# Text queries and keys by column groups, and one double-width load, in a joint image and text attention block

## The chip, the cores and the metric

The kernel runs on one core of a Trainium2 chip. The metric is device time in microseconds (us) of one execution, taken as the median of several. A core has a matrix engine (TensorE, in the profile PE, with its weight loads as PEld), VectorE (DVE), ScalarE (ACT), GpSimd (POOL) and SyncE (SP), which here only issues transfers. Work that goes on together on several engines is ordered by semaphores. TensorE reads from the on-chip memory SBUF (128 partitions) and adds up in eight PSUM banks; VectorE and ScalarE move the sums back to SBUF. Sixteen DMA engines carry data from and to the device memory.

## The reference

Two batches of 256 image tokens and 32 text tokens, width D = 1152, all in bfloat16. Image and text have weights of their own, and meet in one softmax:

```python
mod_i = (_silu(c) @ wmod_img).reshape(B, 6, 1, D)      # shift, scale, gate are the first three
hi = _layernorm(x_img) * (1 + sci) + shi               # ht likewise from x_txt, wmod_txt
qi, ki, vi = split(hi @ wqkv_img)                      # qt, kt, vt likewise from ht, wqkv_txt
q = concat([qt, qi], axis=1)                           # k, v likewise
p = softmax(q @ k.T * D ** -0.5)
at, ai = split(p @ v)
out_i = x_img + gai * (ai @ wo_img)
out_t = x_txt + gat * (at @ wo_txt)
```

## The kernel before

Contractions run over D in KT = 9 blocks of 128 rows. Every weight matrix of 1152 by 1152 lies in SBUF as a tile of 128 partitions by 9 by 1152 (2.65 MB), loaded by SP in one to three pieces (`load_w`, line 73). The tiles share a pool of five slots (line 54); a new matrix takes the slot whose earlier readers are done first. The order of all instructions is written out by hand, each engine and each transfer queue runs its own list in that order, and the loads are issued long ahead: from line 433 on they stand as image keys, text shift, text scale, text tokens, text queries, text keys, image gate (in the place of the image values' weights), text values, image output, text gate, text output.

The stages on TensorE, in order: the image values (`va`), the image shift, the image queries (`qk_img` with `w_q_i`), the image keys (`qk_img` with `w_k_i`), the scores, the text values and gates, the transposed probabilities, the attention's output (`aps`), and the output products (L826 for the image, L799 and L844 for the text).

`qk_img` makes one column block of 128 at a time: nine matmuls over kt, 128 weight columns against 512 image tokens, into one PSUM bank, whose result is cast into `qkTs[blk]`, features on the partitions and tokens along the row. The text work is woven into the image keys by hooks, run ahead of a column block: at 3 the text layer norm, at 6 the strips of text shift and scale (`row_strips`), at 7 the transposes of the text tokens, at 8 the text queries. The text keys follow behind block 8, and then the scores begin (`scores_img`, line 590, one tile for each batch and half of the image queries, over nine feature blocks of image and text keys together; then the text queries' own scores in `scores_txt_and_gate`).

`qk_txt` (line 559) holds 128 columns of the weights still and streams the 64 text tokens past, 81 matmuls for each of queries and keys; two PSUM tiles, one of six and one of three column blocks, are copied out each time.

`mod_strip` (line 399) is the other form that the kernel has for such small products: here the few rows (32) are held still, and the weights stream past. Four matmuls go to four column groups of the array at once, group g with 288 of the 1152 weight columns, and write 32 PSUM partitions each. `strip_cols` then transposes the 128 by 288 result in blocks of 32 by 32 on VectorE, after which partition 32g+j of block m holds feature 128m+32g+j.

PSUM's eight banks are a pool of seven that all matmul results take in turn, and one for small results.

## Time and profile before

| | us |
|---|---|
| median of 3 runs | 114.88 |
| lowest to highest | 114.66 to 114.92 |
| the profiled execution | 114.55 |
| its span, first to last instruction | 112.7 |

The profile is of one execution. Its page gives each engine's busy time and number of instructions, the span cut into 40 slices of 2.8 us (each digit the busy share in tenths), the chain of work that ended last, followed back from the last instruction, and the costliest groups of instructions. A group's row reads: line, engine, operation, output and inputs, shape, count, then busy time, mean duration of one in ns, and the idle time ahead of it. The timeline lists start, length and count of like instructions in a row. Matmuls overlap: one lasts longer than the step to the next, so a row's length contains the last one's tail, and steps are worked out from starts. A few matmul records can be missing.

### The profile page before, as it was taken

The page shows a single profiled execution, that of the slowest core. Times are in us where ns is not written, and L with a number is a line of the kernel's source. Part 1 is how long each engine was busy: PE and PEld are TensorE (multiplying, and loading weights), DVE is VectorE, ACT ScalarE, POOL GpSimd, SP SyncE. Part 2 cuts the span into 40 slices and gives each one's busy share as a digit, 9 for nine tenths or more (in the row PEclk, how much of TensorE's full clock was granted, in tenths as well). Part 3 has the DMA queues.
Part 4 walks back from the last instruction along what each step waited for, and adds up shares of the span by engine and source line. Part 5 has one row for each costly group of instructions (what it writes and reads, how often), then busy time and mean ns, then how long its engine had stood idle before and what let it go on. Part 6 is the DMA issues. An engine that isn't in the chain of part 4 may idle for free.

```text
span 112.7 us, 2837 instructions
## 1 busy us (share of the span) xinstructions
PE 107.6 (95%) x1182; PEld 64.1 (57%) x1191; DVE 76.2 (68%) x151; ACT 36.5 (32%) x83; POOL 28.1 (25%) x62
## 2 busy tenths in 40 slices
PE   5989999999999999999999999999999999999990
PEld 1356665565544444444446558787687565667670
DVE  1699330865499999999999950238657700899971
ACT  4527500471280080730009933024647700001000
POOL 7000120830230000000000161601540460499600
PEclk9999999999999999999999999999999999999999
DMA  3999999999999999999999999999999999994052
GB/s 90 321 376 347 373 373 407 409 413 411 405 410 408 411 410 413 404 412 410 413 410 414 413 403 408 404 398 404 410 407 401 411 422 394 383 371 168 7 192 70
DMA packets 22839, 40.87 MB, mean 363 GB/s; under 512 B 1375, under 2 KB 6635, under 8 KB 22827
## 3 DMA queue, kind: packets, MB, share of 16 engines
q1 hardware_dynamic: 21547, 39.05, 90.4%
q10 hardware_dynamic: 672, 0.77, 2.2%
q0 software_dynamic: 608, 0.88, 2.2%
q8 instruction: 9, 0.15, 0.5%
q14 instruction: 3, 0.02, 0.1%
HBM read 39.36 MB, written 1.34 MB: 361 GB/s over the span
## 4 chain that ended last, share of the span: by engine, by line
PE 89%; DVE 4%; DMA 3%; ACT 1%; issue 1%; ACTq 0%
PE qkps L504 31%; PE ps L826 16%; PE va L256 14%; PE aps L734 5%; PE ps L565 4%; PE sps L594 4%; PE gps L404 3%; DMA x_i<-in_x_img_dram 3%; DVE stats L166 3%; PE ops L844 2%; PE van L268 2%; PE ps L669 2%; PE mps L218 1%; ACT hT_i L202 1%; PE gps L799 1%; PE sps L607 1%
## 5 line engine op out<-in xcount | busy, mean ns | idle before, releaser
L504 PE MATMUL qkps<-hT_i,t 128*128 128x512 bf16 x158 | 35.4, 379 | 0.2
L504 PEld LDWEIGHTS <-t 128*128 128x128 bf16 x162 | 15.6, 98 | 18.7 <-DMA t<-in_wqkv_img_dram 0.3
L466 DVE SCALAR_TENSOR_TENSOR sacc<-w_v_i,mcols,sacc 128x1152 f32<-128x1152 bf16 x16 | 22.7, 1418 | 0.5
L256 PE MATMUL va<-w_v_i,hT_i 128*128 128x512 bf16 x67 | 17.0, 379 | 0.4 <-issue 0.2
L826 PE MATMUL ps<-t,aT 128*128 128x384 bf16 x99 | 16.4, 326 | 0.0
L826 PEld LDWEIGHTS <-aT 128*128 128x128 bf16 x117 | 11.0, 98 | 6.9 <-issue 0.5
L832 DVE TENSOR_TENSOR tmp<-ps,gb 128x384 bf16<-128x384 f32 x11 | 6.0, 548 | 6.5 <-DMA gb<-mod_scratch 6.0
L810 POOL TENSOR_TENSOR w_og<-t,gb 128x384 bf16<-128x384 bf16 x9 | 8.7, 1007 | 5.2 <-DMA gb<-mod_scratch 5.2
L256 PEld LDWEIGHTS <-hT_i 128*128 128x128 bf16 x72 | 6.4, 97 | 5.8 <-issue 0.2
L523 POOL TENSOR_SCALAR mod_txt<-mcols 128x18 f32<-128x18 f32 x2 | 0.6, 275 | 32.4 <-DVE mcols L410 32.4
L166 DVE BATCH_NORM_STATS2 stats<-x_i 128x6 f32<-128x384 bf16 x12 | 5.8, 541 | 2.6 <-DMA x_i<-in_x_img_dram 2.6
L454 ACT ACTIVATE qT<-qkps 128x512 bf16<-128x512 f32 x9 | 4.7, 601 | 6.9 <-PE qkps L504 6.9
L140 PE MATMUL wps<-wz 128*128 128x512 bf16 x15 | 5.6, 536 | 1.2 <-DVE wz L125 1.2
L470 ACT CAST shi<-sacc 128x1152 bf16<-128x1152 f32 x2 | 2.3, 1152 | 13.2 <-DVE sacc L466 13.2
L241 POOL TENSOR_SCALAR hT_i<-hT_i,mod_img 128x128 bf16<-128x128 bf16 (+1 forms) x5 | 2.1, 437 | 14.9 <-ACT hT_i L202 8.5
L747 DVE TENSOR_SCALAR aT<-aps,sv 128x288 bf16<-128x288 f32 (+2 forms) x11 | 4.3, 455 | 2.0 <-PE aps L734 2.0
L833 DVE TENSOR_TENSOR o<-tmp,x_i 128x384 bf16<-128x384 bf16 x11 | 5.3, 479 | 0.4
L565 PEld LDWEIGHTS <-t 128*128 128x128 bf16 x162 | 5.0, 98 | 0.5
L154 DVE CAST kT<-qkps 128x512 bf16<-128x512 f32 x3 | 2.1, 686 | 4.7 <-PE qkps L504 4.7
L565 PE MATMUL ps<-hT_t,t 128*128 128x64 bf16 x162 | 5.0, 193 | 0.0
L734 PE MATMUL aps<-pT,v_i 128*128 128x288 bf16 (+2 forms) x44 | 4.8, 264 | 0.0
L749 ACT ACTIVATE aT<-aps,sv 128x288 bf16<-128x288 f32 (+2 forms) x11 | 4.0, 468 | 2.1 <-PE aps L734 2.1
(150 smaller groups left out, 141.6 us busy)
## 6 DMA issues: line engine op xcount, KB each, us to landing
t<-in_wqkv_img_dram SPq DMA_DIRECT2D x6, 864.0 KB, 13.7
t<-in_wmod_txt_dram SPq DMA_DIRECT2D x2, 2592.0 KB, 18.2
t<-in_wqkv_txt_dram SPq DMA_DIRECT2D x2, 1440.0 KB, 14.3
t<-in_wmod_img_dram SPq DMA_DIRECT2D x3, 864.0 KB, 11.7
t<-in_wqkv_txt_dram SPq DMA_DIRECT2D x3, 864.0 KB, 14.0
t<-in_wo_txt_dram SPq DMA_DIRECT2D x3, 864.0 KB, 15.3
t<-in_wqkv_txt_dram SPq DMA_DIRECT2D x2, 1152.0 KB, 15.0
w_v_i<-in_wqkv_img_dram SPq DMA_DIRECT2D x7, 288.0 KB, 6.7
```

Source lines behind the costliest of these rows:

```text
L140: nc.tensor.matmul(ps[:], lhsT=wz[:, 0:P], rhs=wz[:], start=True, stop=True)
L166: nc.vector.bn_stats(stats[0:np_, k, :], x_ap[:, k * CH:(k + 1) * CH])
L256: nc.tensor.matmul(ps[:], lhsT=hT_i[:, kt, i * P:(i + 1) * P], rhs=w_v_i[:, kt, half * VW:(half + 1) * VW], start=(kt == 0), stop=(kt == K ...
L454: nc.scalar.mul(out_ap, in_ap, SCALE)
L466: nc.vector.scalar_tensor_tensor(saccs[b][:], w_v_i[:, kt, :], ap, saccs[b][:], op0=ALU.mult, op1=ALU.add)
L504: nc.tensor.matmul(pss[j - j0][:], lhsT=wq[:, kt, j * P:(j + 1) * P], rhs=hT_i[:, kt, :], start=(kt == 0), stop=(kt == KT - 1))
L565: nc.tensor.matmul(ps[:, j - j0, :], lhsT=wq[:, kt, j * P:(j + 1) * P], rhs=hT_t[:, kt, :], start=(kt == 0), stop=(kt == KT - 1))
L734: nc.tensor.matmul(bank[:, off:off + c1 - c0], lhsT=lhsT, rhs=rhs, start=(first[id(bank)] == n), stop=(final[id(bank)] == n))
L810: nc.gpsimd.tensor_mul(w_og[:, dt, 0:CH], w_o_i[:, dt, NG0:D], gb[:, B - 1, NG0:D])
L826: nc.tensor.matmul(ps[:, 0:cw], lhsT=aT[:, dt, t0:t0 + P], rhs=rhs, start=(dt == DTS[0]), stop=(dt == DTS[-1]))
L832: nc.vector.tensor_mul(tmp[:, 0:cw], ps[:, 0:cw], gb[:, b, cs])
L833: nc.vector.tensor_add(o[:, cs], tmp[:, 0:cw], x_i[:, i, cs])
```

## The change

Four things are edited.

1. `qk_txt` now works as `mod_strip` does. For queries, then keys, and for each batch, 32 text tokens are held still and the weights stream past in four column groups: nine kt of four matmuls with 288 columns, 144 matmuls in all, into four PSUM tiles.
2. `qk_txt_end` turns each of the four tiles with VectorE's block transpose into a float32 SBUF tile `tcols` (in the place of one of the `sacc` sums) and copies it on ScalarE into the text columns of `qkTs`, the queries multiplied by the scale.
3. Both run in the hook of column block 8, so text keys stand ahead of the last image key block instead of behind it.
4. The text shift and scale weights, neighbours in memory, are loaded as one matrix of 2304 columns in three pieces. The pool shrinks from five slots to three, and a place of two slots' size, `pair`, holds in turn the image scale weights (in its first half), the double-width matrix, and text values with image output.

```diff
-    wpool = ctx.enter_context(tc.tile_pool(name="w", bufs=5))
+    wpool = ctx.enter_context(tc.tile_pool(name="w", bufs=3))
...
-    w_sc_i = wpool.tile([P, KT, D], bf, tag="w", name="w_sc_i")
+    w_sc_i = act.tile([P, 2, KT, D], bf, tag="pair", name="w_sc_i")[:, 0]
...
-    w_sh_t = load_w(wmod_txt, 0)
-    w_sc_t = load_w(wmod_txt, D, K2)
+    w_mod_t = act.tile([P, KT, 2 * D], bf, tag="pair", name="w_mod_t")
+    for k0, k1 in K3:
+        nc.sync.dma_start(w_mod_t[:, k0:k1, :], w_view(wmod_txt)[:, k0:k1, 0:2 * D])
+    w_sh_t, w_sc_t = w_mod_t[:, :, 0:D], w_mod_t[:, :, D:2 * D]
...
-    w_v_t = load_w(wqkv_txt, 2 * D, K3)
-    w_o_i = load_w(wo_img, 0, K2)
+    w_vo = act.tile([P, 2, KT, D], bf, tag="pair", name="w_vo")
+    w_v_t = load_w(wqkv_txt, 2 * D, K3, into=w_vo[:, 0])
+    w_o_i = load_w(wo_img, 0, K2, into=w_vo[:, 1])
...
-    def qk_txt(wq, blk):
-        for j0 in range(0, KT, FG):
-            jn = min(FG, KT - j0)
-            ps = ps_mm.tile([P, FG, NTT], f32, tag="mm")
-            for j in range(j0, j0 + jn):
+    def qk_txt(ws):
+        cols = act.tile([P, len(ws) * B, VC], f32, tag="sacc", name="tcols")
+        todo = []
+        for blk, wt in ws:
+            pss = [ps_mm.tile([P, VC], f32, tag="mm", name="tps") for _ in range(B)]
+            for b in range(B):
                 for kt in range(KT):
-                    nc.tensor.matmul(ps[:, j - j0, :], lhsT=wq[:, kt, j * P:(j + 1) * P], rhs=hT_t[:, kt, :],
-                                     start=(kt == 0), stop=(kt == KT - 1))
-            qk_evac(qkTs[blk][:, j0:j0 + jn, :, NI:NTOK],
-                    ps[:, 0:jn, :].rearrange("p j (b n) -> p j b n", b=B), blk)
-
-    qk_img(w_k_i, 1, 3, hooks={3: txt_norm, 6: row_strips, 7: txt_transposes, 8: lambda: qk_txt(w_q_t, 0)})
-    qk_txt(w_k_t, 1)
+                    wv = wt[:, kt, :].rearrange("p (m g j) -> p g m j", m=KT, g=NGG)
+                    for g in range(NGG):
+                        nc.tensor.matmul(pss[b][32 * g:32 * g + 32, :], lhsT=hT_t[:, kt, NT * b:NT * (b + 1)], rhs=wv[:, g],
+                                         start=(kt == 0), stop=(kt == KT - 1), tile_position=(0, 32 * g))
+                todo.append((blk, b, pss[b]))
+        return cols, todo
+
+    def qk_txt_end(cols, todo):
+        for n, (blk, b, ps) in enumerate(todo):
+            nc.vector.transpose(cols[:, n, :], ps[:])
+            src = cols[:, n, :].rearrange("p (k t) -> p k t", t=NT)
+            dst = qkTs[blk][:, :, b, NI:NTOK]
+            if blk == 0:
+                nc.scalar.mul(dst, src, SCALE)
+            else:
+                nc.scalar.copy(dst, src)
+
+    qk_img(w_k_i, 1, 3, hooks={3: txt_norm, 6: row_strips, 7: txt_transposes,
+                                   8: lambda: qk_txt_end(*qk_txt(((0, w_q_t), (1, w_k_t))))})
```

More of the change, by code (lines that the diff above doesn't have):

```diff
@@ L71, in w_view, with load_w @@
         return src.rearrange("(kt p) n -> p kt n", p=P)
-    def load_w(src, c0, ksplits=((0, KT),), home=None):
-        t = wpool.tile([P, KT, D], bf, tag="w", name="t") if home is None else act.tile([P, KT, D], bf, tag=home, name="w_home")
+    def load_w(src, c0, ksplits=((0, KT),), home=None, into=None):
+        t = into if into is not None else wpool.tile([P, KT, D], bf, tag="w", name="t") if home is None else act.tile([P, KT, D], bf, tag=home, name="w_home")
         for (k0, k1) in ksplits:
@@ L555, in txt_transposes @@
                                  mod_t[:, 0, k0:k1, :].unsqueeze(3).to_broadcast([P, k1 - k0, B, NT]))
-    FG = 6
-    def qk_txt(wq, blk):
-        for j0 in range(0, KT, FG):
-            jn = min(FG, KT - j0)
-            ps = ps_mm.tile([P, FG, NTT], f32, tag="mm")
-            for j in range(j0, j0 + jn):
-                for kt in range(KT):
-                    nc.tensor.matmul(ps[:, j - j0, :], lhsT=wq[:, kt, j * P:(j + 1) * P], rhs=hT_t[:, kt, :],
-                                     start=(kt == 0), stop=(kt == KT - 1))
-            qk_evac(qkTs[blk][:, j0:j0 + jn, :, NI:NTOK],
-                    ps[:, 0:jn, :].rearrange("p j (b n) -> p j b n", b=B), blk)
-    qk_img(w_k_i, 1, 3, hooks={3: txt_norm, 6: row_strips, 7: txt_transposes, 8: lambda: qk_txt(w_q_t, 0)})
-    qk_txt(w_k_t, 1)
+    def qk_txt(ws):
[4 more added lines that the diff above has]
+            for b in range(B):
+                for kt in range(KT):
+                    wv = wt[:, kt, :].rearrange("p (m g j) -> p g m j", m=KT, g=NGG)
[15 more added lines that the diff above has]
+                                   8: lambda: qk_txt_end(*qk_txt(((0, w_q_t), (1, w_k_t))))})
     qpos = [[0, P, 2 * P], [NT, NT + P, 0]]
```

## The prediction

> **What bounds the kernel now.** I read the page's busy time and its slices first, then the chain that ended last in order of time, then TensorE's timeline around the changed lines, and last the issue and landing of the weight loads.

> ```profile
> span 112.7 us, 2837 instructions
> PE 107.6 (95%) x1182; PEld 64.1 (57%) x1191; DVE 76.2 (68%) x151; ACT 36.5 (32%) x83; POOL 28.1 (25%) x62
> ...
> DMA  3999999999999999999999999999999999994052
> GB/s 90 321 376 347 373 373 407 409 413 411 405 410 408 411 410 413 404 412 410 413 410 414 413 403 408 404 398 404 410 407 401 411 422 394 383 371 168 7 192 70
> ```

> TensorE is busy in every slice, and the DMA engines are too until about 101 us, at some 410 GB/s. So two resources are nearly full, and a change can only pay as far as the second lets it. The chain says which one sets the end:

> ```profile
> 65.36 1.94 PE qkps L504 x9
> 67.30 2.36 PE ps L565 x81
> 69.66 0.22 PE qkps L504
> 69.88 0.05 issue
> 69.93 1.67 PE qkps L504 x7
> 71.61 2.36 PE ps L565 x81
> 73.97 4.43 PE sps L594 x36
> ```

> The reader is to see that text queries (81 matmuls), the ninth group of image keys (one record of its nine is missing), text keys (81 more) and the scores follow on TensorE with no wait. The whole chain is TensorE in this way from 9.46 to 109.96 us, so time saved here shows in full unless a load is late. TensorE's timeline gives starts (each group's length includes the tail of its last matmul):

> ```profile
> 60.14 2.39 PE L404 MATMUL gps<-t,sT 128*32 128x288 bf16 x72
> ...
> 65.20 2.10 PE L504 MATMUL qkps<-hT_i,t 128*128 128x512 bf16 x9
> ...
> 71.44 2.52 PE L565 MATMUL ps<-hT_t,t 128*128 128x64 bf16 x81
> ...
> 101.59 2.38 PE L844 MATMUL ops<-t,aT 128*32 128x288 bf16 x72
> 103.90 0.82 PE L826 MATMUL ps<-t,aT 128*128 128x384 bf16 x4
> ```

> L404 is the form that the change gives the text products: 128*32 weights, the same strided view of 288 weight columns, four column groups side by side.

> **The matmuls.** I measure from the start of the last matmul of image-key group 7 (65.20 + 2.10 - 0.38 = 66.92) to the first score matmul, 73.83: 6.91 us now. The change takes out 162 matmuls and puts in 144, which is 36 rounds of four. At L404, 18 rounds start within 2.39 - 0.29 = 2.10 us, 17 steps of 0.123 us; L844's 72 give the same, the 36 at L799 0.125. Matmuls start round by round while earlier ones are still finishing, at full granted clock (1.000).

> The new stretch: into the column groups, 0.31 (the last matmul before L404 starts at 59.83, L404 at 60.14; a plain step there is 0.216, so the switch costs 0.09); 35 steps of 0.123, 4.31; out of them, 0.22 (last matmul of L844 at 103.68, next at 103.90); group 8, nine steps of 0.2155, 1.94. Sum 6.78, against 6.91: **-0.13 us**. Before, entering and leaving L565 cost no switch. Bounds: with L799's step the gain is 0.06; without any cost of a switch (the entry to L565, a plain 0.216) it would be 0.32. I take 0.13, since L404 reads the same view.

> [...] Here all four groups use all 128 rows; were each round to last L404's whole 0.286 us, 36 rounds would take 10.3 us and the run 120.7. L404's loads and its 0.123 us step contradict that, so the sum keeps 0.123.

> **Evacuations.** Four go (0.49, 0.33 and 0.32 us on ScalarE, 0.56 on VectorE). In come four block transposes on VectorE and four copies on ScalarE (first the group of the one block transpose that the kernel has, its mean in ns behind its total; then VectorE's timeline):

> ```profile
> L410 DVE STREAM_TRANSPOSE mcols<-gps 128x288 f32<-128x288 f32 x2 | 0.8, 456 | 0.0
> ```
> ```profile
> 71.64 0.69 DVE L154 CAST kT<-qkps 128x512 bf16<-128x512 f32 x1 [4.74 <-PE qkps L504]
> ```

> That is 4 x 0.456 = 1.82 us, in a stretch where VectorE waits 4.74 us. A copy of 288 elements lies between L454's 0.33 us for 192 and L581's 0.50 for 288: 4 x 0.45 = 1.8 us on ScalarE, idle there too. The strided target may cost more; even doubled the copies end by 73.5. The strip of keys for batch 1 is done last: its matmuls end at about 71.9, transposed by 72.4, copied by 72.9, and read first by the third score tile at 75.9. Batch 0's keys are copied by 71.8 and read at 73.70. Queued behind the copies on ScalarE is only the first exponential (75.62); nothing on the path pays.

> One cover does go. The cast of image-key group 8 lay under 2.4 us of text matmuls; now scores follow at once. It runs from 73.70 + 0.19 = 73.89 to 74.58, and the ninth score matmul, its first reader, is due at 73.70 + 8 x 0.122 = 74.67. Margin 0.09 us; the nearest VectorE-to-TensorE handover, at 7.76 to 7.81 in the chain, took 0.05. Cost 0, at worst some 0.1; anything that holds VectorE longer than the margin costs one for one.

> **Loads and slots.** SP's queue keeps its order and its 24 weight pieces from the image queries' on, three of them (before: 9, 5 and 4 row blocks of 2304-byte rows) now 3, 3 and 3 blocks with 4608-byte rows. No issue count changes. The double-width matrix needs the image scale's slot, whose last reader ends at 19.6, ten before the issue at 29.43. The text-value weights now wait for both strips' readers (62.5) instead of one, up to 0.6 us later than their issue at 61.99. Behind them on SP stand the image output, text gate and text output weights, then stores from 99.42. A piece issued at 59.62 landed 14.4 us later, so over 10 us are queued in the engines and this costs nothing; were that cover gone, 0.6 us would reach the text values. The gate's and output's slots come free at 69.4 and 71.7, before their issues at 75.67 and 78.56. Text-key weights, read from 69.4 instead of 71.44, have landed at 67.4.

> What is late next are two last pieces (SP's issues at line 76, their starts and the time from issue to landing):

> ```profile
> L76 SPq DMA_DIRECT2D t<-in_wqkv_txt_dram x2: 2015/2056/2098, 64.7 to 66.9; - x2
> ...
> DMA to landing us min/median/max: 14.0/14.0/14.0
> ```
> ```profile
> L76 SPq DMA_DIRECT2D t<-in_wo_txt_dram x2: 2100/2110/2119, 84.8 to 87.0; - x2
> ...
> DMA to landing us min/median/max: 15.3/15.3/15.3
> ```

> Text values land at 66.88 + 14.0 = 80.87; the matmul that reads them is due at 79.76 + 6 x 0.218 = 81.07, then 0.13 earlier: 0.07 left. The text output's piece lands at 102.24 and is due at 101.59 + 6 x 0.123 = 102.33, then 102.20: a wait of 0.04 if the stream stands still. For the wider rows there is no such load here. Nearest rows, from the trace's packet records: 128 packets of 4608 bytes on the POOL queue, 181 ns each; 2304-byte ones on SP's, 93 ns each, 187 for two. 72 wide packets per engine at 6 ns less make the stream 0.4 us earlier. The other end: 2048-byte packets on the POOL queue took 85.5 ns, 383 GB/s against 410, which over 5.31 MB would be 0.9 us later. I take the first, the same size, which leaves no wait.

> [...]

> **Sum.** The profiled execution took 114.55 us, 0.33 under the median of 114.88; less 0.13 it is 114.42. Carried to the median: **114.75 us**. Its own range, with 0.06 and 0.32 as ends and the runs' spread, is 114.55 to 114.9.

> **Rivals.**
> 1. *Faster by the loads.* The unprofiled runs (114.66 to 114.92) are all longer than the profiled one. If late weights hold TensorE there (margins of 0.20 and 0.09 are small), a stream 0.4 us earlier gives back most of 0.33: 114.4. Against: the waits view of this execution shows 0.3 us on a weight load only, at 30.8 us, ahead of the change.
> 2. *Given back.* Score nine waits 0.1 for its cast, or the text output weights 0.04: 114.85 to 114.9.
> 3. *Slower: wide rows.* At the 383 GB/s of the other row the text values come 0.9 us late, less 0.07: 114.75 + 0.83 = 115.6. It decides from a delay of 0.20 us (gain and margin used up), and beyond 0.43 (3% of these 5.31 MB) the loss can be told. Against: the 4608-byte row.
> [...]

> **How the numbers follow.** Under 0.2%, 0.23 us, can't be told from no change here. Chances: forecast 0.42 (0.09 of it beyond 0.2% faster, 0.32 within, 0.01 slower), rival 1 0.28 (0.27 faster, 0.01 within), rival 2 0.12 (0.10 within, 0.02 slower), rival 3 0.17 and rival 4 0.01, both slower. Faster 0.36, same 0.43, slower 0.21. The range reaches down to rival 1 with a little spread, 114.3, and up into rival 3, 115.3, leaving out its upper half.

> **What would show it.** Right: 36 rounds at 0.123 us ahead of group 8, the first score matmul about 6.78 us after group 7's last, no wait at the ninth, text-value and text-output pieces landing up to 0.4 us earlier, the tail shifted by 0.13. Wrong: TensorE idle before L594's ninth matmul or before the text-value or text-output matmuls on a load, a step over 0.125, a dip in GB/s between 40 and 55 us or after 62.

## The result and the profile after

The changed kernel took 115.02 us (median of 22 runs, 114.72 to 115.48) against 114.75 us for the kernel before beside it (22 runs, 114.57 to 115.33). The ratio is 1.0022, with a 95% interval of 1.0012 to 1.0032: a loss of some 0.25 us where a gain of 0.13 us was forecast. It lies inside the stated range and on the other side of no change.

The page of the changed kernel opens as the one before did, TensorE (95% busy) and the DMA engines (382 to 427 GB/s in slices 7 to 35) both full; its third part also counts a queue that the prediction passed over, nine transfers of instructions:

```profile
span 113.2 us, 2811 instructions
PE 107.8 (95%) x1173; PEld 62.7 (55%) x1173; DVE 76.8 (68%) x154; ACT 37.1 (33%) x84; POOL 28.0 (25%) x62
...
q8 instruction: 9, 0.15, 0.5%
```

TensorE's timeline around the changed lines (start, length, line, form, count):

```profile
65.67 1.67 PE L507 MATMUL qkps<-hT_i,t 128*128 128x512 bf16 x7
67.27 4.59 PE L569 MATMUL tps<-t,hT_t 128*32 128x288 bf16 x144
71.80 2.12 PE L507 MATMUL qkps<-hT_i,t 128*128 128x512 bf16 x9
73.75 1.02 PE L608 MATMUL sps<-kT,qT 128*128 128x288 bf16 x7
```

The last matmul of group 7 starts at 65.67 + 1.67 - 0.38 = 66.96, the first score matmul at 73.75: 6.79 us against 6.91 before. The edited stretch is 0.12 us shorter. VectorE's and ScalarE's timelines show what took the place of the four evacuations:

```profile
68.61 0.48 DVE L576 STREAM_TRANSPOSE tcols<-tps 128x288 f32<-128x288 f32 x1 [1.67 <-PE tps L569]
...
71.92 0.48 DVE L576 STREAM_TRANSPOSE tcols<-tps 128x288 f32<-128x288 f32 x1 [0.62 <-PE tps L569]
73.95 0.69 DVE L154 CAST kT<-qkps 128x512 bf16<-128x512 f32 x1 [1.55 <-PE qkps L507]
```
```profile
72.43 0.43 ACT L582 CAST kT<-tcols 128x288 bf16<-128x288 f32 x1 [0.67 <-DVE tcols L576]
```

The last transpose and the last copy are done at 72.86, and the cast of group 8 ends at 74.64. Score matmuls go on in steps of 0.122 to 0.123 us through the ninth, as before, so nothing waits there.

Two stages on, TensorE's timeline shows the loss. These are the last matmuls of the text values' narrow columns and the first transpose of the probabilities:

```profile
82.02 0.22 PE L641 MATMUL gps<-w_vo,hT_t 128*32 128x128 bf16 x2
82.03 0.22 PE L646 MATMUL gps<-w_home,sT 128*32 128x128 bf16 x2
82.46 0.23 PE L641 MATMUL gps<-w_vo,hT_t 128*32 128x128 bf16 x2 [0.20 <-issue]
82.46 0.23 PE L646 MATMUL gps<-w_home,sT 128*32 128x128 bf16 x2
82.52 0.22 PE L649 MATMUL gps<-svn,selS 128*32 128x128 bf16 x2
82.68 0.29 PE L692 MATMUL pk<-ident,pb 128*128 128x128 bf16 x2
```

A round of four follows the last by 0.056 us everywhere else in this stretch; here it takes 0.43. The releaser is "issue": neither the weight load nor the matmul has a semaphore to wait for. In the kernel before the same place reads

```profile
82.10 0.22 PE L627 MATMUL gps<-t,hT_t 128*32 128x128 bf16 x2
...
82.15 0.22 PE L627 MATMUL gps<-t,hT_t 128*32 128x128 bf16 x2
...
82.36 0.28 PE L678 MATMUL pk<-ident,pb 128*128 128x128 bf16 x2
```

By stages, from the starts of first matmuls in each kernel's timeline (us):

```
                                        before   after
first transpose of image tokens           7.81    7.84
 to the first image query product        23.11   23.10
 to the first score matmul               42.92   42.81   the edited stretch lies here
 to the first probability transpose       8.54    8.93   not edited
 to the first text output matmul         19.23   19.23
 to the end of the last matmul            8.36    8.36
span                                    112.73  113.21
```

So 0.11 is gained and 0.39 lost, in a stage that the change does not touch. With 0.03 at the start the last matmul ends 0.31 later. Another 0.16 comes behind it, in the closing steps of the program (from the last matmul's end to the span's end 2.79 us before, 2.95 after); the parts of the change below show to which of them this belongs.

### The profile page after: what moved, and what is told of

Its sections match the earlier page's. It is cut to its first block, busy times and chain, and to the rows that moved or that the text cites. A ratio compares the mean times of both kernels' runs of the same rounds, so it can differ in the third digit from the quotient of the medians.

```text
span 113.2 us, 2811 instructions
## 1 busy us (share of the span) xinstructions
PE 107.8 (95%) x1173; PEld 62.7 (55%) x1173; DVE 76.8 (68%) x154; ACT 37.1 (33%) x84; POOL 28.0 (25%) x62
## 4 chain that ended last, share of the span: by engine, by line
PE 90%; DVE 4%; DMA 3%; issue 0%
PE qkps L507 31%; PE ps L840 16%; PE va L256 14%; PE aps L748 5%; PE tps L569 4%; PE sps L608 4%; PE gps L404 3%; DMA x_i<-in_x_img_dram 3%; DVE stats L166 3%; PE ops L858 2%; PE van L268 2%; PE ps L683 2%; PE mps L218 1%; PE gps L813 1%; PE tp L209 1%; PE sps L621 1%
## 5 line engine op out<-in xcount | busy, mean ns | idle before, releaser
L507 PEld LDWEIGHTS <-t 128*128 128x128 bf16 x162 | 15.6, 98 | 18.9 <-issue 0.4
L256 PE MATMUL va<-w_v_i,hT_i 128*128 128x512 bf16 x72 | 17.6, 379 | 0.0
L840 PE MATMUL ps<-w_vo,aT 128*128 128x384 bf16 x99 | 16.4, 326 | 0.0
L824 POOL TENSOR_TENSOR w_og<-w_vo,gb 128x384 bf16<-128x384 bf16 x9 | 8.7, 997 | 4.7 <-DMA gb<-mod_scratch 4.7
L140 PE MATMUL wps<-wz 128*128 128x512 bf16 x15 | 4.9, 485 | 1.2 <-DVE wz L125 1.2
L847 DVE TENSOR_TENSOR o<-tmp,x_i 128x384 bf16<-128x384 bf16 x11 | 4.6, 415 | 0.4
L569 PE MATMUL tps<-t,hT_t 128*32 128x288 bf16 x144 | 4.6, 286 | 0.0
L608 PE MATMUL sps<-kT,qT 128*128 128x288 bf16 x36 | 4.6, 286 | 0.0
L576 DVE STREAM_TRANSPOSE tcols<-tps 128x288 f32<-128x288 f32 x4 | 1.9, 483 | 3.5 <-PE tps L569 3.5
## 6 DMA issues: line engine op xcount, KB each, us to landing
t<-in_wo_txt_dram SPq DMA_DIRECT2D x3, 864.0 KB, 15.3
```

The costliest lines, as they stand in the source:

```text
L140: nc.tensor.matmul(ps[:], lhsT=wz[:, 0:P], rhs=wz[:], start=True, stop=True)
L256: nc.tensor.matmul(ps[:], lhsT=hT_i[:, kt, i * P:(i + 1) * P], rhs=w_v_i[:, kt, half * VW:(half + 1) * VW], start=(kt == 0), stop=(kt == K ...
L507: nc.tensor.matmul(pss[j - j0][:], lhsT=wq[:, kt, j * P:(j + 1) * P], rhs=hT_i[:, kt, :], start=(kt == 0), stop=(kt == KT - 1))
L569: nc.tensor.matmul(pss[b][32 * g:32 * g + 32, :], lhsT=hT_t[:, kt, NT * b:NT * (b + 1)], rhs=wv[:, g], start=(kt == 0), stop=(kt == KT - 1 ...
L608: nc.tensor.matmul(sps[:], lhsT=qkTs[0][:, ft, b, q0:q0 + P], rhs=qkTs[1][:, ft, b, :], start=(ft == 0), stop=(ft == KT - 1))
L824: nc.gpsimd.tensor_mul(w_og[:, dt, 0:CH], w_o_i[:, dt, NG0:D], gb[:, B - 1, NG0:D])
```

## The experiments

The two theories at the start. *Fetch*: TensorE's instructions come from memory in blocks (the page counts nine transfers of instructions), and it ran dry at a block's end; that a block holds 256 was the author's assumption until b_shift110 below. The changed kernel has 36 instructions fewer ahead of this point (144 pairs of weight load and matmul for 162), so the block's end falls elsewhere in the work. *Load* and *strip* rivals: the loss belongs to the double-width load with its shared slots, or to the column-group products.

**Moving the list.** One kernel puts back the 36 places, the other moves the kernel before by 220, which with 36 makes 256. Both do it in the warm-up, whose total width stays:

```diff
-    def warm(n):
-        for _ in range(n):
+    def warm(pieces):
+        for n in pieces:
             ps = ps_mm.tile([P, VW], f32, tag="mm", name="wps")
-            nc.tensor.matmul(ps[:], lhsT=wz[:, 0:P], rhs=wz[:], start=True, stop=True)
+            cut = [VW * k // n for k in range(n + 1)]
+            for c0, c1 in zip(cut, cut[1:]):
+                nc.tensor.matmul(ps[:, c0:c1], lhsT=wz[:, 0:P], rhs=wz[:, c0:c1], start=True, stop=True)
```

> The changed kernel with its 15 warm-up matmuls cut into 33 narrower ones of the same total width, so that every later TensorE instruction stands 36 places further on, as in the kernel before. Instruction-fetch theory (TensorE ran dry at a fixed place in its instruction list, 36 places earlier in the work than before): no gap at 82 us, first transpose of the probabilities 0.1 us earlier than before, ratio to before 0.999 (0.998 to 1.000). Load rival (the double-width load and the shared slots cost the time): unchanged from the changed kernel, 1.002. Strip rival (the column-group products cost it): also 1.002.

> The kernel before, its 15 warm-up matmuls cut into 125 of the same total width: 220 instructions more, which with a period of 256 puts its list where the changed kernel's stands. Fetch theory: the gap of about 0.37 us appears in this kernel too, in the same text-value matmuls (line 627 here), ratio 1.003 (1.002 to 1.004). Load and strip rivals: no gap, 1.000.

Measured: a_shift18 115.04 us against 114.89, ratio 1.0006 (0.9987 to 1.0025), stage 8.54; b_shift110 115.45, ratio 1.0052 (1.0032 to 1.0071), stage 8.93. The chain of waits in order of time, first of a_shift18, then of b_shift110:

```profile
82.63 0.05 PE gps L643 x2
82.68 0.01 PE gps L648 x2
82.69 0.05 PE gps L651 x2
82.74 0.67 PE pk L694 x10
```
```profile
82.34 0.01 PE gps L634 x2
82.35 0.21 issue
82.56 0.23 PE gps L629 x2
82.79 0.01 PE gps L634 x2
```

The gap goes from the changed kernel and comes to the kernel before, though no text product, load or slot was edited in either. The times follow less well than the gaps. a_shift18 was forecast at 0.999; its interval holds that, and no change too. b_shift110 lost 0.56 us, with an interval from 0.37 to 0.82, where at most 0.46 was forecast and the gap is 0.39; in its profile the text output also waits 0.18 us for its third weight piece. Whether cutting the warm-up into 125 costs anything of its own is not shown.

**One part at a time.** strips_only is the kernel before with `qk_txt`, `qk_txt_end` and the hook of the change; wide_only is the changed kernel with the text products of before.

```diff
# strips_only, against the kernel before
-    qk_img(w_k_i, 1, 3, hooks={3: txt_norm, 6: row_strips, 7: txt_transposes, 8: lambda: qk_txt(w_q_t, 0)})
-    qk_txt(w_k_t, 1)
+    qk_img(w_k_i, 1, 3, hooks={3: txt_norm, 6: row_strips, 7: txt_transposes,
+                                   8: lambda: qk_txt_end(*qk_txt(((0, w_q_t), (1, w_k_t))))})
```

> The kernel before with the column-group text products alone, loads and slots as they were. Its TensorE list is the changed kernel's. Fetch theory: gap at 82 us, ratio 1.002. Load rival: no loss, 0.999. Strip rival: 1.002.

> The changed kernel with the text products of before: double-width load and shared slots alone. Fetch theory: TensorE's list is that of before, so no gap, 1.000 (0.999 to 1.001), weights after the wide load landing 0.2 to 0.4 us earlier. Load rival: 1.002 or more. Strip rival: 1.000.

Measured: strips_only 115.04 us, 1.0015 (0.9998 to 1.0032), stage of the edited stretch 42.80, stage behind it 8.74, a gap of 0.20; wide_only 114.93, 0.9999 (0.9981 to 1.0018), stages 42.92 and 8.59, of which 0.05 is a wait for the last piece of the text values' weights (landed at 81.45). For the gap the load rival falls: it comes with the text products alone. That it is their count of instructions, not their work, is what the shifts show.

The closing steps are another matter. From the last matmul's end to the end of the span the five profiles without the double-width load show 2.78 to 2.80 us, and ten of the eleven profiles with it 2.95 to 2.96 (a_quiet, below, which loads four matrices fewer, 2.75). So the 0.16 us belongs to the load and its slots, though no load is late there. What differs is one of SyncE's closing instructions, named DRAIN. These rows have the shortest, median and longest of its three in ns and the first and last start in us, first of the kernel before, then of the changed one:

```profile
L899 SPq DRAIN  x3: 7/7/13, 111.9 to 112.5; - x3
```
```profile
L913 SPq DRAIN  x3: 7/13/109, 112.2 to 112.9; - x3
```

SyncE's list is one instruction shorter with the wide load, 81 in the profile against 82, and in all these fifteen profiles the late one is the 80th: without the wide load a semaphore wait, whose delay of some 0.3 us lies beside other engines' closing work, with it the DRAIN behind that wait. In a_quiet, with 71, none is late. This looks like the effect found on TensorE, on another engine's list. It is not shown: no kernel moved SyncE's list alone, and in neither of the two profiles does a transfer on an instruction queue start between 105 and 113 us.

In the timed runs the double-width load by itself is worth nothing that can be told; the interval of wide_only holds both 0 and the 0.16 us.

**How far, and what the DMA engines have to do with it.** Smaller and larger shifts of the same kind (2, 6 and 30 more pieces), and a kernel in which the weight stream ends early:

```diff
# a_quiet, against the changed kernel
-    w_ga_i = load_w(wmod_img, 2 * D, K2, home="V")
+    w_ga_i = w_v_i
...
-    w_o_i = load_w(wo_img, 0, K2, into=w_vo[:, 1])
-    w_ga_t = load_w(wmod_txt, 2 * D)
-    w_o_t = load_w(wo_txt, 0, K3)
+    w_o_i = w_q_t
+    w_ga_t = w_q_t
+    w_o_t = w_k_t
```

> The changed kernel with 2 of its warm-up matmuls cut in two, 4 instructions more. Fetch theory: the request goes out while TensorE passes the scores, 0.061 us per instruction, instead of the dense stretch; 4 places bring it forward by 0.24 us and the place that needs it by 0.03, so a gap of about 0.17 us (0.05 to 0.30) is left of 0.39: first score matmul to first transpose 8.7 us (8.54 without a gap, 8.93 with all of it). Rival, that only a large shift or the cut warm-up itself matters: 8.93.

> The changed kernel with 6 warm-up matmuls cut in two, 12 instructions more. Fetch theory: request 0.7 us earlier, gap gone, 8.54 us from the first score matmul to the first transpose; time 0.999 of before (0.9975 to 1.0005). Rival: gap left, 1.002.

> The changed kernel with its 15 warm-up matmuls cut into 45, 60 instructions more. Fetch theory: gap at 82 us gone too (8.54), unless another dense stretch now meets its own block's end; 0.999 of before (0.9975 to 1.0005). Rival: 1.002.

> The changed kernel without the loads of image gate, image output, text gate and text output weights, whose products use other weights already there; the weight stream ends near 74 us. TensorE's list is the changed kernel's, place for place. If the full DMA engines make the fetch slow: its 16 KB take well under 0.9 us, it starts at once, and the gap shrinks to 0 to 0.15 us (8.54 to 8.7 from first score matmul to first transpose). If the fetch is slow by itself: 8.93 as before.

Measured: a_shift2 114.66 us in one run, a_shift6 114.88 against 114.79, 0.9999 (0.9986 to 1.0012), a_shift30 114.91, 1.0005 (0.9987 to 1.0023), a_quiet 114.76 in one run; stage 8.54 in all four. Four places were enough, where 0.17 us of gap had been expected to stay. In a_quiet TensorE's list stands exactly as in the changed kernel, and the gap is gone with the traffic:

```profile
DMA  3999999999999999999999999600001800220142
GB/s 64 363 364 343 371 376 405 412 410 412 403 413 405 421 422 425 411 424 409 412 410 412 412 395 409 236 12 6 0 7 30 235 6 0 104 104 6 38 153 70
```

Its slices 27 to 31, from some 73 to 87 us, move next to nothing. The trace's packet records give the start of the 16,384-byte transfer on the instruction queue that belongs to this place. Set beside the first score matmul, all profiles fall into one order:

```
kernel           places moved   transfer starts after     gap at 82 us
                 (mod 256)      first score matmul, us    us
a_quiet                0             3.64                  0
wide_only             36             4.26                  0
before                36             4.28                  0
b_shift2              40             4.36                  0
a_shift30             60             4.65                  0
a_shift18             36             4.69                  0
a_add18               36             4.70                  0
a_shift6              12             5.64                  0
a_shift2               4             5.95                  0
s_shift2               4             5.97                  0
a_shift2_timed         4             6.02                  0
a_add2                 4             6.09                  0.11
strips_only            0             6.23                  0.20
after_again            0             6.25                  0.25
after                  0             6.39                  0.39
b_shift110             0             6.42                  0.39
```

Whoever starts by 6.02 us has no gap, and every later start has one about as long as the delay. (s_shift2 counts for little here: a late load, shown below, held TensorE before it came to this place.) The transfer itself took 0.96 to 1.10 us in all of them, where the expectation for a_quiet has well under 0.9; TensorE goes on some 2.3 us after its start (80.14 to 82.46 in the changed kernel). a_quiet against the changed kernel puts the wait for the full DMA engines at 6.39 - 3.64 = 2.75 us.

The place in the list settles it. Counting weight loads and matmuls from the trace, the first to come late is number 1,721 in the changed kernel, its second profile, strips_only and a_add2, where another matmul stands at that number, and number 1,977 = 1,721 + 256 in b_shift110.

The same count shows why 36 places matter. From number 1,465 to 1,721, one block, the kernel before takes 4.45 us (by the starts of its weight loads), and a_quiet, whose list is the changed kernel's without the gap, 3.51 us: the block now begins later among the scores and ends among the short rounds. When a block is asked for is not shown; its transfer starts 0.73 us behind number 1,465 in the kernel before (78.11 against 77.38) and 1.63 behind it in the changed kernel (80.14 against 78.51). On the author's assumption that it is asked for about where the block ahead begins, the transfer has 0.94 us less. In a_quiet, where the traffic is gone, it starts at 3.64 us, 1.1 us ahead of number 1,465.

**What closing it is worth.** The changed kernel again, with a shift of four on the same chip, and the products alone with that shift:

> The changed kernel as it is, beside the next two on one chip. Fetch theory: 8.93 us from first score matmul to first transpose, time 1.002 of before (1.001 to 1.004).

> The changed kernel with 2 warm-up matmuls cut in two (4 instructions more). Fetch theory: no gap, 8.54 us, so the 0.12 us of the text products is kept: 0.999 of before (0.9975 to 1.0005), and 0.3 to 0.4 us under the changed kernel. Rival, that the gap at 82 us is only where the profile shows a loss that lies elsewhere in unprofiled runs: 1.002 like the changed kernel.

> The column-group text products alone, loads and slots as before, with the same 4 instructions more. Fetch theory: no gap, 8.54 us, 0.999 of before (0.9975 to 1.0005). If the double-width load is worth something of itself, this one is slower than the last by 0.1 us or more.

Measured: after_again 114.91 us against 114.90, 1.0003 (0.9989 to 1.0016), gap 0.25, both less than forecast; a_shift2_timed 114.66, 0.9982 (0.9967 to 0.9997), no gap; s_shift2 114.87, 0.9992 (0.9979 to 1.0006). All eleven runs of after_again took longer than a_shift2_timed's median, and the medians lie 0.25 us apart, so on this chip the gap shows in time too. s_shift2 is 0.21 us slower than a_shift2_timed, which by its expectation would speak for the double-width load; but the two intervals overlap, and its profile, of its slowest run, has a stage of 8.96 us, not 8.54. It has no gap, but a wait of another kind (TensorE's timeline):

```profile
79.97 1.47 PE L682 MATMUL ps<-t,hT_t 128*32 128x512 bf16 x24
81.68 0.83 PE L682 MATMUL ps<-t,hT_t 128*32 128x512 bf16 x12 [0.24 <-DMA t<-in_wqkv_txt_dram]
```

The last piece of the text values' weights landed at 81.64; the matmul was due at 79.97 + 6 x 0.218 = 81.28. This is the late load that the prediction feared, in a kernel without the wide load.

The shifted kernels' times left a doubt: the more the warm-up was cut, the less they gained. Hence a control that has no gap to close, and shifts with added matmuls behind a whole warm-up:

```diff
# a_add2 and a_add18, n = 2 and 18
     warm(11)
+    wps = ps_mm.tile([P, VW], f32, tag="mm", name="wps")
+    for k in range(n):
+        nc.tensor.matmul(wps[:, 16 * k:16 * k + 16], lhsT=wz[:, 0:P], rhs=wz[:, 0:16], start=True, stop=True)
```

> Control: the kernel before with 2 of its warm-up matmuls cut in two. It has no gap at 82 us to close. Fetch theory: no change, 1.000 (0.9985 to 1.0015), 8.54 us from first score matmul to first transpose. If the cut itself gave the 0.16 us: 0.9985 or less.

> The changed kernel with 2 matmuls of 16 columns added behind the whole warm-up (4 instructions more, about 0.05 us in a stretch where TensorE waits for the layer norm). Fetch theory: gap closed as with the cut of 2, 8.54 us, 0.999 of before (0.9975 to 1.0005). If the cut was what counted: 8.93 or 1.002.

> The changed kernel with 18 matmuls of 16 columns added behind the whole warm-up (36 instructions more, about 0.45 us, of which TensorE's wait for the layer norm hides most). Fetch theory: 8.54 us, 0.999 to 1.001 of before. If cutting the warm-up cost what the 18 cuts lost, this one is 0.2 us faster than they were.

Measured, against 114.89: b_shift2 114.80, 1.0002 (0.9988 to 1.0016), so the cut of two gives nothing by itself; a_add2 114.77, 0.9993 (0.9980 to 1.0007), with 0.11 of gap left; a_add18 114.88, 0.9999 (0.9984 to 1.0013), 8.54. The chain of a_add2 shows the gap at other matmuls, the round before the last, at the same number of the list:

```profile
82.31 0.05 PE gps L644 x2
82.36 0.16 PE gps L649 x2
82.52 0.01 PE gps L644 x2
```

a_add18 and a_shift18 differ by 0.16 us, within their intervals, so whether cutting costs anything at 18 stays open. Over the six timed shifts of the changed kernel, cut or added, the ratios run from 0.9982 to 1.0006. Closing the gap brings the change back to about the time of before, and the stages say why it is not less: 0.12 us gained in the edited stretch, 0.16 lost in the closing steps. Only the interval of a_shift2_timed lies below 1, ending at 0.9997; it is one of six, and no stage of its profile shows where a gain over the kernel before would come from, so it may be luck.

## Why the prediction was wrong

- **The matmuls: right.** 6.79 us against the 6.78 worked out, 0.12 gained against 0.13. The 144 started within 4.59 - 0.29 = 4.30 us. Entering cost 67.27 - 66.96 = 0.31 and leaving 0.22, as L404 and L844 had shown. Rival 4 of the chances, rounds that each last their whole 0.286 us (120.7 us), was rightly left at one in a hundred: no run shows such rounds, the step was 0.123 us.
- **Evacuations: right.** 0.48 us for a transpose (0.456 expected), 0.43 to 0.44 for a copy (0.45), and the cover of 0.09 us at the ninth score matmul held.
- **Loads: right in kind.** The double-width matrix made the stream 0.32 us earlier: the piece ahead of it landed 0.25 us later than before (41.44 against 41.19), its own last piece 0.07 earlier (54.03 against 54.10). The other profiles agree: from the landing of the last image-key piece but one to that of the matrix it is 14.70 to 14.83 us in the eleven with the wide load and 15.04 in the five without. The rows had given 0.4. Rival 3 falls with the measurement. Text values landed at 80.80, due at 80.98; text output at 102.15, due after the gap at 102.64.
- **Rival 1: its evidence was misread.** The profiled run was shorter than the others not because those wait for weights that the wide load speeds up, but because the first 31 us vary: the first transpose of image tokens started between 7.72 and 8.48 us in the fifteen profiles other than that of before, and the way from there to the image queries took 22.79 to 23.70, with waits for the image scale weights. The two ends belong to every kernel, with or without the wide load. Late weights do occur behind it (two of the five profiles without the wide load, s_shift2 and b_shift110; one of the eleven with it, 0.15 us at the text output in wide_only), but the profiles are too few to say that the wide load prevents them.
- **The step that failed** is in the first part: "time saved here shows in full unless a load is late". One more supply feeds TensorE, its instructions, and 36 fewer of them was counted as time alone. The page had the line (nine transfers on an instruction queue), and no term of the sum or rival was made of it. It cost 0.39 us in the first profile and 0.25 in the second. The same sentence, with "the tail shifted by 0.13", also puts the closing steps at nothing: they grew by 0.16 us, with the double-width load, and why SyncE is late there stays open.
- **What the terms add up to.** Less the 0.12 that was right, gap and closing steps make 0.43 us in the first profile and 0.29 in the second. The timed runs lost less: 0.25 us (0.14 to 0.37) in the first comparison, 0.03 (from 0.13 gained to 0.18 lost) in the second. A profile is one execution, and the stages of the others were not recorded, so the rest of the difference is not explained. The gap was the longer the later the transfer started (0.25 us at 6.25 behind the first score matmul, 0.39 at 6.39), which may be why the two comparisons differ. That the measured time lies inside the stated range is luck, not a merit of the sum: the range was made wide for rivals 1 and 3, and neither is what happened.

## What to carry to other kernels

When an edit changes the number of instructions of a busy engine, everything behind it shifts against the blocks in which its instructions arrive: here by 36, against late places 256 apart. Look at where the block ends fall. TensorE ran dry here, for up to 0.39 us, where one fell into a stretch of very short instructions, eight in 0.056 us, with the DMA engines at some 400 GB/s, and "issue" (0.20 us) on an instruction without a semaphore is how it showed. Such a row alone is no proof: the 0.16 us of "issue" at 29.78 in the chain of the kernel before stands where a matmul record is missing (67 of line 256's 72 are there), while the weight load started at 29.71. Before judging such an edit by a few tenths of a microsecond, move the list by a few places with instructions that cost next to nothing (the four of b_shift2: 1.0002, 0.9988 to 1.0016), and compare again.
